# The first unit's row maxima over eight PSUM tiles, and the second unit's leading maxima ahead of the main loop

## The chip, the cores and the metric

One core of one Trainium2 chip runs the kernel. The metric is device time in microseconds (us), as the median of several executions; smaller is better. The engines are named as in the profile: PE (TensorE, matrix products, with PEld for its weight loads), DVE (VectorE), ACT (ScalarE), POOL (GpSimd) and SP (SyncE, which here only issues transfers). A queue such as ACTq or SPq is an engine's part that issues DMA transfers.

## The reference

Two independent results stand side by side in the output. `a` is a state-space convolution: a kernel `K` is made from 448 x 256 complex exponentials over 2048 positions, and the input is convolved with it. `b` is full attention with 16 heads of 28 columns over 2048 rows.

```python
K = 2.0 * jnp.einsum("dn,dnl->dl", C, P).real        # a: P = exp((A dt) l)
y = irfft(rfft(u_t, L2) * rfft(K, L2), L2)[:, :, :L] + u * D_skip

scores = jnp.einsum("bhqd,bhkd->bhqk", q, k) * scale  # b
p = softmax(scores, axis=-1)
b = (einsum("bhqk,bhkd->bhqd", p, v) ...) @ wo
out = jnp.concatenate([a, b], axis=-1)
```

## The kernel before

**Units and steps.** The 16 heads are four groups of four (`G`, `HG`), and the queries four blocks of 512 (`NQ`, `CQ`). A group with a query block is a unit `u`, 16 in all. The main loop (line 1045) has 256 steps `s`, 16 of them to a unit, one for each 128 keys (`kt`). A step makes for each of four heads a score tile (`s_mm`, line 753: a matmul into `pss`, then an exp on ACT into `p`), and adds the last step's `p` times `v` to the output tile `po` (`pv_step`, line 760).

**Row maxima.** An exp needs the largest score of its query row taken off beforehand. That maximum travels inside the matmul: two rows of the q tile `qhat` (one holds the rounded value, one the rest) hold minus the maximum, beside two rows of ones in `khat`. So a unit's maxima must be finished, and its row put into `qhat`, before the unit's first score matmul. A unit has 16 blocks `i`, each for one head `j` and 128 queries, and a block looks at 2048 keys in four columns `kc` of 512 (`max_mm`, line 187). For columns 0 and 1 a pair is used, max(a, b) = b + relu(a - b): `kc` 0 multiplies with the stored difference of keys, `kdif`, and ACT makes `rl`, the relu; `kc` 1 multiplies with the second half of the keys, and DVE adds `rl` and reduces in one operation. Columns 2 and 3 are matmuls that DVE reduces plainly.

For unit 0 alone, ahead of the loop, columns 2 and 3 are also a pair (`max_pair`, line 173). There is no stored difference for them, so two matmuls into one tile make it, the second with `q_neg`, minus the q tile, which ACT copies ahead of the first block (line 580). A block of unit 0 is then five matmuls, two relus and two pair reductions; a block of any other unit is four matmuls, one relu, one pair reduction and two plain ones.

After the last block `max_join` (line 208) takes the maximum over a block's values, `max_end` (line 212) transposes them on PE and splits them into the two rows `mh`, and `max_put` (line 220) sends these into `qhat` by two transfers, for unit 0 on ACT's queue.

**PSUM.** There are eight banks, one tile of 128 x 512 each. Before the loop they are divided into `ps_w` (3 tiles, `pm`, handed out in turn by `w_tile`, line 125), `ps_t` (2, `pt`), `ps_n` (2, `pn`) and `ps_x` (1, `px`); `pn` and `px` are used by the preparation of the convolution's seeds, whose last work ends at about 195 us. Unit 0's maxima use `pt` and `pm`, five tiles in turn (line 576). In the loop the banks are divided anew: `ps_s` (3, `pss`), `ps_o` (1), `ps_g` (1) and `ps_m` (3, again called `pm`). The relu results `rl` have two buffers, in the pool `kd_p`.

**The order of the work.** Up to line 590 the order of instructions on an engine comes from a scheduler, which starts from the order of the text and may let a later instruction go first. From line 903 on the text's order is kept on all engines (`nc.kept = KEPT["a"]`). There, first the seeds of three convolution blocks are loaded (`load_sd`, line 655; block 0 on ACT's queue, blocks 1 and 2 on SP's), then the first three (`LEAD`) blocks of unit 1's maxima are made (line 906), then ACT copies block 0's seeds `e` and `g` out of `sdb` (`k_seeds`, line 659), and the loop begins. The leading blocks give the loop its distance: step `s` makes the scores of its own unit and block `s + 16 + LEAD` of the maxima (line 1092), with the order in a step written out in `ORDER` (line 34): `m0`, `s0`, `m1`, `s1` and so on. POOL raises the powers of `e` (`e_power`, line 673), which PE multiplies with `g` some steps later (`k_mm`, line 712).

Of the kernel before, what the change touches and what calls it, by code (L numbers as in the profile page):

```python
# [8 lines left out]
F32 = mybir.dt.float32  # L9
F32R = mybir.dt.float32r  # L10
I32 = mybir.dt.int32
AF = mybir.ActivationFunctionType
# [11 lines left out]
HG = H // G  # L24
CQ = 512
# [7 lines left out]
LEAD = 3  # L33
# [57 lines left out]
def body(ctx, tc, a, out):  # L91
    nc = Engines(tc)
# [4 lines left out]
    def pool(stack, name, bufs=1, space=None, side=None):  # L97
        kw = {} if space is None else {"space": space}
        if side:
            kw["side"] = side  # L100
        return stack.enter_context(tc.tile_pool(name=name, bufs=bufs, reuse_waits="tile", **kw))
# [30 lines left out]
    kd_p = pool(att, "kd_p", side="right")  # L132
# [10 lines left out]
    kt_g, kd_g, q_u, m_u, mh_u, o_u, rl_u = {}, {}, {}, {}, {}, {}, {}  # L143
# [26 lines left out]
        for r in rows:  # L170
            nc.sync.dma_start(t[r::4].bitcast(F32), q_d[g][c][r // 2].rearrange("(j p) q -> p j q", j=HG))

    def max_pair(i, kc, ps, q_neg):
        j, t = divmod(i, 4)
        ts = slice(t * 128, (t + 1) * 128)
        pm, kt = ps(), kt_g[0][j]
        if kc == 2:
            nc.tensor.matmul(pm, q_u[0][:, j, ts], kt[:, 2 * CQ:3 * CQ], start=True, stop=False)
            nc.tensor.matmul(pm, q_neg[:, j, ts], kt[:, 3 * CQ:], start=False, stop=True)
            rl_u[0, i] = kd_p.tile([128, CQ], F32, name="rl", bufs=2)  # L180
            nc.scalar.activation(rl_u[0, i], pm, AF.Relu)
        else:
            nc.tensor.matmul(pm, q_u[0][:, j, ts], kt[:, 3 * CQ:], start=True, stop=True)
            rl = rl_u.pop((0, i))
            nc.vector.tensor_tensor_reduce(rl, pm, rl, 1.0, -3.0e38, ALU.add, ALU.max, m_u[0][:, j, t, 1:2])

    def max_mm(u, i, kc, ps=w_tile):

        if i == 0 and kc == 0:
            m_u[u] = q_p.tile([128, HG, 4, 3], F32, name="mx", bufs=2)  # L190
        j, t = divmod(i, 4)
        pm = ps()
        q, kt = q_u[u][:, j, t * 128:(t + 1) * 128], kt_g[u // NQ][j]
        mx = m_u[u][:, j, t, max(kc - 1, 0):max(kc - 1, 0) + 1]
        if kc == 0:
            nc.tensor.matmul(pm, q, kd_g[u // NQ, j], start=True, stop=True)
            rl_u[u, i] = kd_p.tile([128, CQ], F32, name="rl", bufs=2)
            nc.scalar.activation(rl_u[u, i], pm, AF.Relu)
        elif kc == 1:
            kb = kt.rearrange("p (c s n) -> p c s n", c=NQ, s=2)[:, :2, 1, :]  # L200
            nc.tensor.matmul(pm.rearrange("p (c n) -> p c n", c=2), q, kb, start=True, stop=True)
            rl = rl_u.pop((u, i))
            nc.vector.tensor_tensor_reduce(rl, pm, rl, 1.0, -3.0e38, ALU.add, ALU.max, mx)
        else:
            nc.tensor.matmul(pm, q, kt[:, kc * CQ:(kc + 1) * CQ], start=True, stop=True)
            nc.vector.tensor_reduce(mx, pm, axis=AX.X, op=ALU.max)

    def max_join(u, n=3):
        m_u[u, 1] = q_p.tile([128, HG * 4], F32, name="m1", bufs=2)
        nc.vector.tensor_reduce(m_u[u, 1], m_u[u].rearrange("p a b c -> p (a b) c")[:, :, :n], axis=AX.X, op=ALU.max)  # L210

    def max_end(u, ps):
        nc.tensor.transpose(ps[:16, :128], m_u[u, 1], ident)
        mh = q_p.tile([16, 2, 128], F32R, name="mh")
        nc.vector.tensor_scalar(mh[:, 0, :], ps[:16, :128], -1.0, None, op0=ALU.mult)
        nc.vector.scalar_tensor_tensor(mh[:, 1, :], ps[:16, :128], -1.0, mh[:, 0, :].bitcast(F32),
                                       op0=ALU.mult, op1=ALU.subtract)
        mh_u[u] = mh

    def max_put(u, queue=nc.sync):  # L220
        for i in range(2):
            queue.dma_start(q_u[u][4 * (DH + i):4 * (DH + i) + 1, :, :].rearrange("p h (t q) -> p (h t) q", t=4).bitcast(F32),
                                mh_u[u][:, i, :].bitcast(F32))


    with ExitStack() as st:
# [6 lines left out]
        ps_t = pool(st, "ps_t", 2, PSUM)  # L233
        ps_n = pool(st, "ps_n", 2, PSUM)
        ps_x = pool(st, "ps_x", 1, PSUM)
# [47 lines left out]
        half_pi = s_p.tile([128, 1], F32, name="half_pi")  # L283
# [289 lines left out]
                    load_v(0, c)  # L573
                kept_g.pop()()
        xst.close()
        more = [lambda: ps_t.tile([128, CQ], F32, name="pt")] * 2 + [w_tile] * 3
        n_st = ExitStack()
        q_neg = pool(n_st, "n_p").tile([128, HG, CQ], F32R, name="q_neg")
        for j in range(HG):
            nc.scalar.activation(q_neg[:, j], q_u[0][:, j].bitcast(F32), AF.Copy, scale=-1.0)  # L580
        for i in range(16):
            for kc in range(4):
                f, kw = (max_mm, (0, i, kc)) if kc < 2 else (max_pair, (i, kc))
                f(*kw, more[(4 * i + kc) % 5], *([q_neg] if kc > 1 else []))
        nc.scalar.activation(half_pi[:1], half_pi[:1], AF.Exp)
        n_st.close()
        max_join(0, 2)
        max_end(0, ps_t.tile([128, CQ], F32, name="pt"))
        max_put(0, nc.scalar)
        sst.close()  # L590


# [62 lines left out]
    def load_sd(b, queue=nc.sync):  # L655
        sds[b] = g_p.tile([128, SDF], F32, name="sdb", bufs=4)
        queue.dma_start(sds[b], sd_d[b // BO][b % BO])

    def k_seeds(b):

        if b not in es:
            es[b] = e = g_p.tile([128, 2, 16, N2], F32, name="e", bufs=2)
            nc.scalar.activation(e[:, :, :, :8], sds[b][:, :F_G].rearrange("p (c h e) -> p c h e", c=2, e=8), AF.Copy)
        else:
            g = g_p.tile([128, 2, 16, N1], F32, name="g", bufs=2)
            nc.scalar.activation(g[:, :, :, :4], sds[b][:, F_G:F_Z].rearrange("p (c h e) -> p c h e", c=2, e=4), AF.Copy)
            egs[b] = es.pop(b), g
# [235 lines left out]
    nc.kept = KEPT["a"]  # L903
    for b in range(3):
        load_sd(b, nc.sync if b else nc.scalar)
    for i in range(LEAD):
        for kc in range(4):
            max_mm(1, i, kc)
    k_seeds(0)
    k_seeds(0)  # L910

# [133 lines left out]
    for s in range(NS):  # L1045
# [25 lines left out]
        ps = []  # L1071
# [97 lines left out]
```

## Time and profile before

| what | value |
|---|---|
| median of 3 runs | 1283.33 us |
| lowest, highest | 1280.13, 1284.64 us |
| the profiled execution's own time | 1284.67 us |
| its span | 1282.8 us |
| PE busy | 1223.7 us, 95% of the span |
| DVE busy | 925.5 us, 72% |
| ACT busy | 967.8 us, 75% |
| POOL busy | 843.4 us, 66% |
| unit 0's pair reductions | from 196.04 to 224.87 us |
| unit 1's leading blocks on DVE | from 228.46 to 234.96 us |
| first score matmul | 234.41 us |

All times inside the profile count from the span's start; the time of the execution is a little longer than its span. A row of the timeline has the start, the duration, the engine, the operation with `out<-in` by the program's names, the number of merged instructions, and in brackets how long the engine had been idle and what ended that. A row of busy times by stretch has the stretch, then the busy time and the instructions of each engine, the clock that PE was granted as a share of the full one, and the share and rate of the DMA engines. An operation on DVE that also returns a maximum is two rows, CUSTOM_DVE_ANT_0 and a short DVE_READ_ACCUMULATOR2_ANT. Because a helper records every operation, all have the line 75, so tiles and engines tell them apart.

### The profile page before, as it was taken

The numbers are of one execution on the slowest core, as the hardware profiler recorded it, in microseconds if no ns is written. First come the engines' busy times: TensorE is split into PE (matmuls) and PEld (weight loads), VectorE is DVE, ScalarE is ACT, GpSimd is POOL, SyncE is SP. The second block draws the span as 40 slices with busy tenths as digits, with TensorE's granted clock in tenths as the row PEclk, the third lists the DMA queues.
The fourth block names the chain that finished last, engine by engine and source line by source line (L and its number), as shares of the span: only waits on it lengthen the run. The fifth ranks groups of instructions, "written<-read, shape, count | busy, mean of one in ns | idle before, by whom it ended". The sixth has DMA issues, their size and how long they took to land.

```text
span 1282.8 us, 33335 instructions
## 1 busy us (share of the span) xinstructions
PE 1223.7 (95%) x12641; PEld 700.9 (55%) x12641; DVE 925.5 (72%) x2106; ACT 967.8 (75%) x2162; POOL 843.4 (66%) x728
## 2 busy tenths in 40 slices
PE   7988867999999999999999999999999999999987
PEld 5867754455555555555555555555555555544433
DVE  5788877787877787878778888888887645645111
ACT  4978856688888888888888888888887666656452
POOL 2466651798778888877689999989995222324321
PEclk9988888899999999999999999999999999999999
DMA  6767887446664544465533223432324533657665
GB/s 210 263 242 241 265 301 290 127 93 182 172 154 106 156 133 146 128 214 195 169 102 91 61 76 106 149 88 71 83 59 154 175 135 132 205 171 227 194 171 165
DMA packets 200089, 205.36 MB, mean 160 GB/s; under 512 B 95992, under 2 KB 158520, under 8 KB 197880
## 3 DMA queue, kind: packets, MB, share of 16 engines
q1 hardware_dynamic: 199720, 202.87, 51.4%
q8 instruction: 100, 1.64, 0.5%
q10 hardware_dynamic: 208, 0.36, 0.1%
q14 instruction: 61, 0.50, 0.1%
HBM read 120.73 MB, written 82.18 MB: 158 GB/s over the span
## 4 chain that ended last, share of the span: by engine, by line
PE 77%; DVE 7%; ACT 5%; POOL 5%; issue 3%; DMA 2%; SPq 0%; ACTq 0%; POOLq 0%; DVEq 0%
PE pm L75 44%; PE pss L75 16%; PE po L75 16%; POOL e L75 1%; ACT tri L75 1%; DVE mx L75 1%; ACT rl L75 1%; PE pt L75 1%; POOL qhat L75 1%; DVE sg L75 1%; DVE hl L75 1%; DVE tri L75 1%; POOL x_e L75 1%; DVE px L75 1%; POOL p L75 1%
## 5 line engine op out<-in xcount | busy, mean ns | idle before, releaser
L75 ACT ACTIVATE p<-pss 128x512 f32<-128x512 f32 x1024 | 561.4, 611 | 112.8 <-PE pss L75 108.5
L75 PE MATMUL pss<-qhat,khat 128*128 128x512 f32 x1024 | 402.7, 399 | 1.5 <-ACT p L75 1.4
L75 DVE TENSOR_REDUCE mx<-pm 128x1 f32<-128x512 f32 x480 | 308.6, 684 | 109.6 <-PE pm L75 107.5
L75 PE MATMUL pm<-khat,qhat 128*128 128x512 f32 x749 | 326.4, 439 | 5.3 <-ACT rl L75 3.0
L75 POOL TENSOR_TENSOR e<-e,sdb 128x256 f32<-128x256 f32 x168 | 201.9, 1202 | 108.1 <-ACT e L75 62.4
L75 PE MATMUL po<-p,v 128*32 128x512 f32 x2048 | 269.1, 594 | 0.0
L75 POOL TENSOR_TENSOR e<-e,eu 128x256 f32<-128x256 f32 x168 | 248.0, 1476 | 13.2
L75 PEld LDWEIGHTS pm<-khat,qhat 128*128 128x128 f32 x749 | 141.4, 189 | 201.3 <-ACT p L75 52.0
L75 DVE CUSTOM_DVE_ANT_0 rl<-pm,rl 128x512 f32<-128x512 f32 x259 | 178.4, 689 | 71.6 <-ACT rl L75 68.4
L75 PEld LDWEIGHTS pss<-qhat,khat 128*128 128x128 f32 x1024 | 190.4, 188 | 46.1 <-issue 10.8
L75 POOL TENSOR_TENSOR eu<-e,sdb 128x256 f32<-128x256 f32 x168 | 202.0, 1202 | 0.0
L75 POOL TENSOR_TENSOR p<-pr,pr 64x448 f32<-64x448 f32 x64 | 73.1, 1142 | 160.4 <-PE pm L75 135.2
L75 ACT ACTIVATE rl<-pm 128x512 f32<-128x512 f32 x259 | 157.1, 607 | 12.7 <-PE pm L75 7.9
L75 DVE TENSOR_TENSOR g<-g,zg 128x128 f32<-128x128 f32 x392 | 162.2, 414 | 3.4
L75 PE MATMUL pm<-kdif,qhat 128*128 128x512 f32 x249 | 101.1, 406 | 8.5 <-DVE xn L75 6.6
L75 PE MATMUL pm<-xh,khat 112*128 112x512 f32 x256 | 87.0, 422 | 9.2 <-DVE kb L75 4.4
L75 DVE TENSOR_TENSOR zg<-g,zg 128x128 f32<-128x128 f32 x224 | 87.9, 393 | 5.1
L75 PEld LDWEIGHTS pm<-e,g 128*32 128x32 f32 x3584 | 57.2, 109 | 43.8 <-issue 16.1
L75 DVE TENSOR_TENSOR pr<-pm,ub 128x448 f32<-128x448 f32 x64 | 37.0, 620 | 56.2 <-PE pm L75 41.8
L75 PE MATMUL pm<-e,g 128*32 128x64 f32 x3584 | 73.0, 222 | 1.9 <-POOL e L75 1.9
L75 ACT ACTIVATE y<-pm 128x448 f32<-128x448 f32 x48 | 26.5, 553 | 58.2 <-PE pm L75 34.1
L75 ACT ACTIVATE ub<-pm 128x224 f32<-128x224 f32 (+1 forms) x96 | 38.8, 450 | 39.9 <-PE pm L75 37.6
(134 smaller groups left out, 1465.5 us busy)
## 6 DMA issues: line engine op xcount, KB each, us to landing
sdb<-sd SPq DMA_DIRECT2D x55, 336.0 KB
qhat<-q SPq DMA_DIRECT2D x64, 256.0 KB
khat<-k SPq DMA_DIRECT2D x64, 256.0 KB
sd<-sg SPq DMA_DIRECT2D x8, 1456.0 KB
k<-hl SPq DMA_DIRECT2D x16, 512.0 KB
mw<-in_mw SPq DMA_DIRECT2D x16, 512.0 KB
sd<-qhat SPq DMA_DIRECT2D x8, 896.0 KB
yu_d<-ub SPq DMA_DIRECT2D x64, 112.0 KB
```

The source lines that it names most:

```text
L75: i = f(*args, **kw)
```

## The change

Unit 0's maxima go over all eight PSUM tiles instead of five, in the order `pt`, `pm`, `pt`, `pm`, `pn`, `pm`, `pn`, `px`, and a block's columns are taken in the order 0, 2, 1, 3 instead of 0, 1, 2, 3, so that both relus come ahead of both reductions. The relu buffers of columns 2 and 3 get a place of their own: three in the pool of `q_neg` (`n_p`), beside the two in `kd_p` that columns 0 and 1 and unit 1 use. The text of unit 0's end (join, transposition, row) now stands ahead of unit 1's three leading blocks, which leave the part whose order is kept (line 906) and come before line 590, over the same eight tiles; the pool of `q_neg` closes after them. The seed loads, which stood ahead of the leading blocks, now follow them in the text.

```diff
-    def max_pair(i, kc, ps, q_neg):
+    def max_pair(i, kc, ps, q_neg, rl_p):
...
-            rl_u[0, i] = kd_p.tile([128, CQ], F32, name="rl", bufs=2)
-            nc.scalar.activation(rl_u[0, i], pm, AF.Relu)
+            rl_u[0, i, 1] = rl_p.tile([128, CQ], F32, name="rl", bufs=3)
+            nc.scalar.activation(rl_u[0, i, 1], pm, AF.Relu)
...
-        more = [lambda: ps_t.tile([128, CQ], F32, name="pt")] * 2 + [w_tile] * 3
+        p_t, p_n, p_x = (lambda p=p, n=n: p.tile([128, CQ], F32, name=n) for p, n in ((ps_t, "pt"), (ps_n, "pn"), (ps_x, "px")))
+        more = [p_t, w_tile, p_t, w_tile, p_n, w_tile, p_n, p_x]
...
         for i in range(16):
+            for n, kc in enumerate((0, 2, 1, 3)):
+                ps = more[(4 * i + n) % 8]
+                max_mm(0, i, kc, ps) if kc < 2 else max_pair(i, kc, ps, q_neg, n_p)
+        nc.scalar.activation(half_pi[:1], half_pi[:1], AF.Exp)
+        max_join(0, 2)
+        max_end(0, p_t())
+        max_put(0, nc.scalar)
+        for i in range(LEAD):
             for kc in range(4):
-                f, kw = (max_mm, (0, i, kc)) if kc < 2 else (max_pair, (i, kc))
-                f(*kw, more[(4 * i + kc) % 5], *([q_neg] if kc > 1 else []))
-        nc.scalar.activation(half_pi[:1], half_pi[:1], AF.Exp)
+                max_mm(1, i, kc, more[(4 * i + kc + 1) % 8])
         n_st.close()
-        max_join(0, 2)
-        max_end(0, ps_t.tile([128, CQ], F32, name="pt"))
-        max_put(0, nc.scalar)
...
     for b in range(3):
         load_sd(b, nc.sync if b else nc.scalar)
-    for i in range(LEAD):
-        for kc in range(4):
-            max_mm(1, i, kc)
     k_seeds(0)
```

More of the change, by code (lines that the diff above doesn't have):

```diff
@@ L179, in max_pair @@
             nc.tensor.matmul(pm, q_neg[:, j, ts], kt[:, 3 * CQ:], start=False, stop=True)
-            rl_u[0, i] = kd_p.tile([128, CQ], F32, name="rl", bufs=2)
-            nc.scalar.activation(rl_u[0, i], pm, AF.Relu)
+            rl_u[0, i, 1] = rl_p.tile([128, CQ], F32, name="rl", bufs=3)
+            nc.scalar.activation(rl_u[0, i, 1], pm, AF.Relu)
         else:
             nc.tensor.matmul(pm, q_u[0][:, j, ts], kt[:, 3 * CQ:], start=True, stop=True)
-            rl = rl_u.pop((0, i))
+            rl = rl_u.pop((0, i, 1))
             nc.vector.tensor_tensor_reduce(rl, pm, rl, 1.0, -3.0e38, ALU.add, ALU.max, m_u[0][:, j, t, 1:2])
@@ L575, in body @@
         xst.close()
-        more = [lambda: ps_t.tile([128, CQ], F32, name="pt")] * 2 + [w_tile] * 3
+        p_t, p_n, p_x = (lambda p=p, n=n: p.tile([128, CQ], F32, name=n) for p, n in ((ps_t, "pt"), (ps_n, "pn"), (ps_x, "px")))
+        more = [p_t, w_tile, p_t, w_tile, p_n, w_tile, p_n, p_x]
         n_st = ExitStack()
-        q_neg = pool(n_st, "n_p").tile([128, HG, CQ], F32R, name="q_neg")
+        n_p = pool(n_st, "n_p")
+        q_neg = n_p.tile([128, HG, CQ], F32R, name="q_neg")
         for j in range(HG):
```

## The prediction

> **What bounds the kernel now.** I read the page first, for the chain of work that ended last and the groups, then the busy times by stretch, then the timelines of DVE, PE and ACT around 195 to 235 us, where the changed lines run.
>
> ```profile
> PE 77%; DVE 7%; ACT 5%; POOL 5%; issue 3%; DMA 2%; SPq 0%; ACTq 0%; POOLq 0%; DVEq 0%
> ...
> L75 PE MATMUL pm<-e,g 128*32 128x64 f32 x3584 | 73.0, 222 | 1.9 <-POOL e L75 1.9
> ```
>
> 77% of the chain is TensorE's own work. The second row matters below: in the whole run PE waited 1.9 us for GpSimd's powers. All operations stand under the helper's line, 75, so I go by tiles.
>
> ```profile
> core 0: us, PE busy (x) PEld busy (x) DVE busy (x) ACT busy (x) POOL busy (x), PEclk, DMA share, GB/s
> 196.06:203.30 7.24, 6.98 (x15) 4.38 (x15) 4.10 (x13) 5.46 (x10) 0.76 (x1) 0.50 1.02 391
> 203.30:224.90 21.60, 18.03 (x62) 10.13 (x60) 17.35 (x52) 14.30 (x25) 0.00 (x0) 0.99 0.66 234
> 224.90:234.40 9.50, 7.10 (x14) 3.64 (x15) 5.88 (x15) 2.30 (x5) 1.08 (x2) 0.64 0.65 208
> 234.40:300.00 65.60, 65.46 (x685) 34.65 (x687) 53.47 (x126) 55.22 (x123) 58.32 (x47) 1.00 0.43 110
> 300.00:960.00 660.00, 655.64 (x7866) 366.28 (x7859) 543.41 (x1296) 553.41 (x1272) 572.17 (x450) 1.00 0.44 125
> ```
>
> From 234.40 us on, the main loop, PE is busy 65.46 of 65.60 us and then 655.64 of 660 at a granted clock of 1.00, in an order written out by hand. So the loop has a length of its own, and whatever lets it begin earlier ends the kernel earlier by as much. The change touches only the three stretches before it: the first unit's maxima while PE's clock is at 0.50 (7.24 us), the same at full clock (21.60 us, no engine full), and the passage to the loop (9.50 us), where no engine is full at the clock it could have.
>
> ```profile
> 196.04 0.69 DVE L75 CUSTOM_DVE_ANT_0 rl<-pt,rl 128x512 f32<-128x512 f32 x1 [1.06 <-ACT rl L75]
> ...
> 203.29 0.69 DVE L75 CUSTOM_DVE_ANT_0 rl<-pm,rl 128x512 f32<-128x512 f32 x1 [0.58 <-ACT rl L75]
> ...
> 206.80 0.69 DVE L75 CUSTOM_DVE_ANT_0 rl<-pt,rl 128x512 f32<-128x512 f32 x1
> 207.41 0.08 DVE L75 DVE_READ_ACCUMULATOR2_ANT mx<- 128x1 f32 x1
> 207.83 0.69 DVE L75 CUSTOM_DVE_ANT_0 rl<-pm,rl 128x512 f32<-128x512 f32 x1 [0.34 <-ACT rl L75]
> ...
> 224.18 0.69 DVE L75 CUSTOM_DVE_ANT_0 rl<-pm,rl 128x512 f32<-128x512 f32 x1 [0.34 <-ACT rl L75]
> 224.79 0.08 DVE L75 DVE_READ_ACCUMULATOR2_ANT mx<- 128x1 f32 x1
> 224.91 0.19 DVE L75 TENSOR_REDUCE m<-mx 128x16 f32<-128x32 f32 x1
> 225.55 0.28 DVE L75 TENSOR_SCALAR mh<-pt 16x128 fp32r<-16x128 f32 x1 [0.45 <-PE pt L75]
> 225.86 0.28 DVE L75 SCALAR_TENSOR_TENSOR mh<-pt,mh 16x128 fp32r<-16x128 f32 x1
> 228.46 0.69 DVE L75 CUSTOM_DVE_ANT_0 rl<-pm,rl 128x512 f32<-128x512 f32 x1 [2.32 <-ACT rl L75]
> 229.08 0.08 DVE L75 DVE_READ_ACCUMULATOR2_ANT mx<- 128x1 f32 x1
> 229.08 1.28 DVE L75 TENSOR_REDUCE mx<-pm 128x1 f32<-128x512 f32 x2
> ```
>
> The custom operation is the reduction of a pair (max of pm plus rl): 32 of them for unit 0, two for each of 16 blocks, the first at 196.04, the seventh at 203.29, the 32nd at 224.18. Where the next is ready, one follows after 0.61 us (206.80 to 207.41); but the one after that waits 0.34 us for ACT's rl. From the seventh to the 32nd it is (224.18 - 203.29) / 25 = 0.84 us for each. At 228.46 unit 1's three leading blocks begin, one pair reduction and two plain reductions (1.28 us) each.
>
> ```profile
> 206.77 0.39 PE L75 MATMUL pm<-khat,q_neg 128*128 128x512 f32 x1
> 207.00 0.40 PE L75 MATMUL pt<-khat,qhat 128*128 128x512 f32 x1
> ...
> 228.48 0.79 PE L75 MATMUL pm<-khat,qhat 128*128 128x512 f32 x1 [2.05 <-ACT rl L75]
> ...
> 234.41 0.41 PE L75 MATMUL pss<-qhat,khat 128*128 128x512 f32 x1
> ```
>
> ```profile
> 225.91 1.25 ACTq L75 DMA_DIRECT2D qhat<-mh  x2
> 227.19 0.59 ACTq L75 DMA_DIRECT2D sdb<-sd  x1
> 227.83 0.60 ACT L75 ACTIVATE rl<-pm 128x512 f32<-128x512 f32 x1 [3.69 <-DMA qhat<-mh]
> ...
> 232.84 0.41 ACT L75 ACTIVATE e<-sdb 128x256 f32<-128x256 f32 x1
> ...
> 235.11 1.09 ACT L75 ACTIVATE p<-pss 128x512 f32<-128x512 f32 x2
> ```
>
> ACT stood 3.69 us idle while it held the row's two transfers and the first seed's load ahead of the leading blocks' first rl. I measure the passage from the 32nd pair reduction, L = 224.18: row issued at L+1.7, seed load at L+3.0, first leading rl at L+3.65, first leading reduction at L+4.3, first score matmul at L+10.2, first exp at L+10.9.
>
> **The change, part by part.**
>
> *Eight tiles and the order 0, 2, 1, 3.* Nothing is added or removed: 80 matmuls, 32 rl, 32 pair reductions as before. Full-clock matmuls follow each other after 0.23 us (206.77 to 207.00), five a block, 1.17 us; DVE needs 2 x 0.61 = 1.22; ACT's rl take 0.60, two a block 1.20. All three are below the 1.68 us (2 x 0.84) that a block takes now, so the time goes in waiting for a tile or an rl buffer to come back. With eight tiles a block's tile is wanted again two blocks later, 2.4 us, and the chain matmul 0.40, rl 0.60, reduction 0.69 is 1.7: it fits. The rl buffers go from two in all to two and three. The floor is DVE's 0.61 a reduction; with three engines within 5% of one another I don't expect the floor. 0.72, the middle of 0.61 and 0.84, is the other end; I take 0.65, nearer the floor. From the seventh reduction, 203.29 + 25 x 0.65 = 219.54: **4.6 us earlier** (5.6 at the floor, 2.9 at 0.72). Before the seventh I expect no gain: at clock 0.50 five matmuls take twice 1.17 us, 2.3, PE is busy 6.98 of 7.24 us, and the start waits on ACT behind the seeds, which the diff leaves alone.
>
> *q_neg stays where it is; the relu buffers move to its pool*, which closes after the leading blocks instead of before the row. No instruction; the readers of those buffers are done by L+0.7 either way, ahead of everything that takes their place. Cost nothing; without that cover at most one reduction, 0.69.
>
> *The leading blocks ahead of the loop.* Twelve matmuls, three rl, nine reductions, no DMA. They are moved past the row's ACT transfers, past the load of seed 0 (ACT queue) and seeds 1 and 2 (SP), and past nothing on POOL. In the part where they now stand the order on an engine isn't held to the text. That such reordering happens shows in a row: the Exp that loads the table is written behind the first unit's blocks and ran long ahead of them.
>
> ```profile
> L75 ACT ACTIVATE half_pi<-half_pi x1: 202/202/202, 179.6 to 179.6; 1x1 f32<-1x1 f32 x1
> ```
>
> So I expect the three rl ahead of the row's transfers, which only become ready at L+1.7. DVE then has: last reduction 0.7, join 0.2, row 0.56, and 3 x 0.61 + 3 x 1.28 = 5.7 of leading reductions, together L+7.2, no longer L+4.3 + 5.7. A reduction that stands ahead of the row's two operations delays the row by 0.7 at most, and behind the row waits only the first score matmul, which has slack: issued at L+1.7, it released ACT 1.9 us later (225.91 to 227.83), so it is there at L+4.3.
>
> What is late next is seed 0. Its load is issued at L+3.0 as now. ACT takes e and g from it ahead of the loop's first rl and exp, in the written order, so all exps queue behind that landing. Bounds for the landing: 1.9 us after issue as with the row, or 5.65, since at 232.84 e ran without a wait. Middle 3.8: L+6.8. Then e 0.41, g 0.3 at most 0.41 like e, rl 0.60, 1.3 together: first exp at L+8.1 instead of L+10.9, **2.8 us** (1.0 to 4.7 between the bounds). POOL's first power follows e, which stands 2.3 us ahead of the first exp now and 1.3 then, 1.0 later against the loop; PE waited 1.9 us for powers in the whole run, and I set the cost at nothing, 1.9 if that cover goes.
>
> *The loop's first tiles* take the banks of the leading blocks; the last reader is done at L+7.2, before the first exp. Nothing, or one plain reduction, 0.64.
>
> Sum: 4.6 + 2.8 = **7.4 us**. The profiled execution itself took 1284.67 us (span 1282.8), 1.3 above the median; its own time would become 1277.3, and the median 1283.33 becomes **1275.9**.
>
> *The clock.* In the rows the clock is 0.50 for 7.24 us although PE is busy for 6.98 of them, and an idle gap of 2.05 us at 228.48 stands in a stretch that averages 0.64; yet at 234.40 the clock is 1.00. After the change PE has its twelve leading matmuls done early and then waits for the tiles, the row and exp, so the loop's first steps could fall into a slow stretch.
> [...]
>
> **The rivals.**
>
> A. *ACT keeps the written order*: row transfers, then the three rl. The third rl needs the first buffer back at L+5.0, seed 0's load goes out at L+5.6, lands at L+9.4, first exp L+10.7. Gain 4.6 + 0.2: 1278.5. For it: the ACT rows above; against: the table's Exp.
>
> B. *The loop begins at clock 0.50.* PE is then the bound and each such us loses half: up to 7.24 / 2 = 3.6. 1275.9 to 1279.5, most likely about 1278. For it: the 0.64 row; against: 1.00 at 234.40 after a stretch with about as many matmuls as the new one.
>
> C. *The tiles weren't the limit*, so the change doesn't do what it says: ACT, at 1.20 of 1.22 us, passes each delay on, and 0.84 stays. Gain 2.8 only: 1280.5.
>
> D. *Slower.* The freedom that lets the rl go ahead lets a leading matmul go ahead on PE's queue of the first unit's, and it needs unit 1's q.
>
> ```profile
> 205.02 3.44 SPq L75 DMA_DIRECT2D qhat<-q  x4
> ```
>
> Those four loads end issuing at 208.46 and land, by the row's 1.9, at 210.4 or later. A leading matmul placed at 198.0, two microseconds behind the first reduction, would hold PE 12.4 us; less the 7.4, 5.0 us slower: 1288.3. It decides up to 199.1: a later place gives a loss within 0.3%, and one behind 203.0 a gain. Against it: sixteen blocks stand in front in the text, and each freed tile is wanted by one of them first.
>
> E. *More*: with eight tiles PE doesn't stall in the slow stretch and gets its clock half of it, 3.6 us, sooner: 1.6 blocks become 2.8, 1.2 x 1.3 = 1.6 us more, 1274.3.
>
> **How the numbers follow.** Forecast 0.47, A 0.10, B 0.15, C 0.11, D 0.09, E 0.08. A difference of 0.3%, 3.85 us, is about what a measurement of this kernel can tell from no change, so faster means below 1279.5: forecast, A, E and 0.11 of B, 0.76. Same: C and the rest of B, 0.15. Slower: D, 0.09. The bounds alone give gains of 2.9 + 1.0 = 3.9 (1279.4) to 5.6 + 4.7 = 10.3 (1273.0). The range goes down to 1271.5 for E on top of these, and up to 1281.5 to take in C with 1 us of the runs' spread; D is left out.
>
> **What would show it.** Pair reductions of unit 0 about 0.65 us apart from the seventh on and the 32nd near 219.5; no wait of 3.7 us on ACT at the row; the first leading reduction within 1.5 us of the 32nd; first exp near 227.6 and e<-sdb just ahead of it; clock 1.00 from there. Wrong would make it: a 32nd reduction later than 222, leading rl behind the row's transfers (A), 0.50 in the loop's first 7 us (B), a score matmul or a first-unit matmul waiting for q (D), or a loop longer than now by more than 1 us from first exp to end.

## The result, and the profile after

The changed kernel takes 1278.63 us (median of 20 runs, 1276.68 to 1283.24), the kernel before, in 20 runs beside it, 1282.09. The ratio is 0.998, 95% interval 0.9973 to 0.9987: 2.6 us gained (1.7 to 3.5), where 7.4 were forecast. The ratio is taken over all the runs; the two medians alone lie 3.5 us apart. The profiled execution took 1278.61 us, its span is 1276.8. The kernel before took 1284.67 us in its profiled execution, 2.6 above its median, so the two profiles lie further apart than the runs.

I split both spans at the same four events. T1 and L are the starts of the first and the 32nd pair reduction of unit 0 (L as in the prediction). Exps are counted from 0, so exp 8 is the first of the loop's third step (the expectations call it the eighth).

| stretch, us | before | after | difference |
|---|---|---|---|
| start to T1 | 196.04 | 194.39 | -1.65 |
| T1 to L (unit 0) | 28.14 | 23.81 | -4.33 |
| L to exp 0 | 10.94 | 11.45 | +0.51 |
| exp 0 to exp 8 | 5.51 | 5.96 | +0.45 |
| exp 8 to the end | 1042.18 | 1041.20 | -0.98 |

I don't count the first and the last row to the change. T1 follows ACT's last work for the seeds (`sg`, at 195.01 before and 193.36 after), and ACT's order ahead of T1 is the same; PE makes some of unit 0's matmuls earlier, into `pn` and `px`. T1 spreads from 192.79 to 194.77 in ten profiles with the changed kernel's unit 0, from 192.94 to 196.04 in five with the old order. The last row's difference lies within the spread of all the profiles (1040.55 to 1043.40). So of the 6.0 us between the two spans 3.4 lie where the change works. Unit 0 gave about what was forecast (4.6), though not where it was forecast; the passage to the loop, forecast 2.8 shorter, became a little longer.

The busy times by stretch come next, first after, then before, split where the granted clock changes:

```profile
194.39:197.64 3.25, 3.25 (x7) 1.93 (x7) 2.62 (x7) 2.03 (x4) 0.78 (x1) 0.50 1.00 379
197.64:224.94 27.30, 21.86 (x80) 13.34 (x78) 21.92 (x69) 18.67 (x35) 0.00 (x0) 1.00 0.77 266
224.94:231.77 6.83, 4.36 (x10) 3.38 (x11) 4.40 (x11) 3.12 (x8) 2.47 (x4) 0.50 0.85 252
231.77:300.00 68.23, 67.92 (x752) 36.12 (x754) 54.72 (x130) 56.85 (x126) 61.61 (x49) 1.00 0.42 104
```

```profile
196.04:203.71 7.67, 7.39 (x16) 4.70 (x17) 4.53 (x13) 5.48 (x10) 0.78 (x1) 0.50 1.03 391
...
227.60:234.43 6.83, 5.95 (x11) 3.08 (x12) 5.16 (x12) 2.30 (x5) 1.11 (x2) 0.50 0.90 289
```

In both a stretch of 6.83 us at clock 0.50 lies at the passage. Before, it ended at 234.43, 0.7 us ahead of the first exp (235.11), so the loop ran at full clock. After, the first exp is at 229.65 and the half clock lasts until 231.77: it has moved into the loop.

The timeline of DVE, ACT and PE in the passage after the change:

```profile
218.20 0.69 DVE L75 CUSTOM_DVE_ANT_0 rl<-px,rl 128x512 f32<-128x512 f32 x1
...
221.84 0.69 DVE L75 CUSTOM_DVE_ANT_0 rl<-pt,rl 128x512 f32<-128x512 f32 x1 [1.68 <-ACT rl L75]
...
226.68 0.68 DVE L75 TENSOR_REDUCE mx<-pn 128x1 f32<-128x512 f32 x1
```

```profile
219.93 1.24 ACTq L75 DMA_DIRECT2D qhat<-mh  x2
221.21 1.09 ACT L75 ACTIVATE rl<-pm 128x512 f32<-128x512 f32 x2 [4.07 <-PE pn L75]
222.64 0.60 ACT L75 ACTIVATE rl<-pm 128x512 f32<-128x512 f32 x1 [0.34 <-DVE mx L75]
222.66 0.35 ACTq L75 DMA_DIRECT2D sdb<-sd  x1
228.65 0.42 ACT L75 ACTIVATE e<-sdb 128x256 f32<-128x256 f32 x1 [5.42 <-DMA sdb<-sd]
...
229.65 1.08 ACT L75 ACTIVATE p<-pss 128x512 f32<-128x512 f32 x2
```

```profile
219.26 0.27 PE L75 MATMUL pt<-ident,m 128*16 128x128 f32 x1 [2.26 <-DVE m L75]
219.50 0.47 PE L75 MATMUL pm<-kdif,qhat 128*128 128x512 f32 x1
...
223.80 0.50 PE L75 MATMUL pn<-khat,qhat 128*128 128x512 f32 x1
227.41 0.80 PE L75 MATMUL pm<-kdif,qhat 128*128 128x512 f32 x1 [3.11 <-DVE mx L75]
228.00 0.63 PE L75 MATMUL pss<-qhat,khat 128*128 128x512 f32 x1
228.43 0.63 PE L75 MATMUL pm<-khat,qhat 128*128 128x512 f32 x1
```

L is 218.20. These rows show three holds, one behind another. **The row**: ACT issues the row's transfers at 219.93 and only then the leading blocks' first rl (221.21); and on PE the twelve leading matmuls stand behind the transposition, which waits for the join. The leading reductions run from L+3.6 to L+9.2, not from about L+1 to L+7.2. **The bank**: the loop's first matmul (227.41) had waited 3.11 us for DVE, until the last leading reduction (226.68 and 0.68 long) freed its bank. **The seed**: its load goes out at 222.66 behind the third leading rl, and e, which stands ahead of every exp, waits for it until 228.65, 6.0 us behind the issue.

### The profile page after: what moved, and what is told of

The parts are those of the page before. It is cut to its first block, busy times and chain, and to the rows that moved or that the text cites. A ratio compares the mean times of both kernels' runs of the same rounds, so it can differ in the third digit from the quotient of the medians.

```text
span 1276.8 us, 33338 instructions
## 1 busy us (share of the span) xinstructions
PE 1219.3 (95%) x12641; PEld 699.8 (55%) x12641; DVE 925.3 (72%) x2106; ACT 966.9 (76%) x2162; POOL 843.5 (66%) x728
## 4 chain that ended last, share of the span: by engine, by line
PE 77%; DVE 9%; ACT 4%; POOL 4%; issue 3%; DMA 2%; ACTq 0%; SPq 0%; POOLq 0%; DVEq 0%
PE pm L75 43%; PE pss L75 17%; PE po L75 16%; POOL qhat L75 1%; DVE mx L75 1%; DVE sg L75 1%; ACT tri L75 1%; DVE px L75 1%; DVE tri L75 1%; POOL x_e L75 1%; DVE hl L75 1%; DVE qhat L75 1%; PE pt L75 1%; DVE rl L75 1%; POOL p L75 1%
## 5 line engine op out<-in xcount | busy, mean ns | idle before, releaser
L75 PE MATMUL pm<-khat,qhat 128*128 128x512 f32 x737 | 320.2, 435 | 6.1 <-DVE mx L75 1.7
L75 PEld LDWEIGHTS pm<-khat,qhat 128*128 128x128 f32 x737 | 138.6, 188 | 198.2 <-ACT p L75 45.3
L75 DVE CUSTOM_DVE_ANT_0 rl<-pm,rl 128x512 f32<-128x512 f32 x245 | 168.8, 689 | 67.3 <-ACT rl L75 65.2
L75 PE MATMUL pm<-kdif,qhat 128*128 128x512 f32 x240 | 95.9, 400 | 4.2 <-DVE mx L75 3.1
```

The source lines that it names most:

```text
L75: i = f(*args, **kw)
```

## The experiments

Each kernel ran five to twelve times, beside 21 to 26 runs of the kernel before on the same chip (its medians 1281.25 to 1281.64). Ratios are to that kernel. Unit 0 is T1 to L, and exps count from L; both come from one profiled execution of each kernel, and executions of one kernel lie up to 6.7 us apart. With the row on SP alone the profiled execution was the slowest of seven (1279.81 us, median 1276.99), with all three edits the fastest of five (1273.58, median 1275.09).

| run | ratio (95%) | unit 0 | exp 0 | exp 8 |
|---|---|---|---|---|
| kernel before | 1 | 28.14 | 10.94 | 16.45 |
| changed kernel | 0.998 (0.9973 to 0.9987) | 23.81 | 11.45 | 17.41 |
| unit 0's part alone | 0.9973 (0.9962 to 0.9985) | 25.84 | 10.96 | 16.49 |
| the same, five tiles | 0.9977 (0.9968 to 0.9986) | 25.05 | 10.96 | 16.84 |
| eight tiles, old order, two rl buffers | 0.9969 (0.9957 to 0.998) | 24.28 | 10.96 | 16.96 |
| the move alone | 1.0005 (0.9996 to 1.0014) | 27.60 | 11.50 | 17.09 |
| change + seed early | 0.998 (0.997 to 0.999) | 25.78 | 10.54 | 17.65 |
| change + row on SP | 0.9966 (0.9953 to 0.9979) | 25.81 | 10.20 | 17.25 |
| change + banks dealt | 0.9981 (0.997 to 0.9991) | 24.05 | 11.33 | 19.13 |
| change + row, seed | 0.9977 (0.9968 to 0.9986) | 23.74 | 9.33 | 16.64 |
| change + seed, banks | 0.9956 (0.994 to 0.9973) | 24.04 | 8.90 | 16.64 |
| change + row, banks | 0.997 (0.996 to 0.998) | 25.82 | 10.53 | 17.21 |
| change + row, seed, banks | 0.9948 (0.9936 to 0.9961) | 23.84 | 7.65 | 13.40 |
| move + row, seed, banks | 0.9977 (0.9967 to 0.9987) | 27.35 | 7.15 | 13.71 |

**The two parts apart.** Theory: unit 0's part carries the gain, and the move gives nothing because the holds above take its place. Rival: both are half as good as forecast. First unit 0's part with the leading blocks back behind the seed loads (the edit is against the changed kernel), then the move with unit 0 as before (against the kernel before; lines left out at the dots):

```diff
-        for i in range(LEAD):
-            for kc in range(4):
-                max_mm(1, i, kc, more[(4 * i + kc + 1) % 8])
...
+    for i in range(LEAD):
+        for kc in range(4):
+            max_mm(1, i, kc)
     k_seeds(0)
```

> Only the first part: unit 0 over eight tiles, the leading blocks back in the kept part behind the seed loads. Theory (the leading blocks' move gave nothing, because their relus stood behind the row's transfers on ACT and seed 0 landed later): first to last pair reduction of unit 0 takes 23.8 us as in the changed kernel (28.1 before), last reduction to first exp 10.9 as before; 3.8 to 4.3 us faster than before, so no worse than the changed kernel. Rival (the move gave its 2.8 us and the loop lost it again): 11.4 or more to the first exp and a slower time than the changed kernel by about 2 to 3 us.

```diff
-        n_st.close()
...
+        more = [p_t, w_tile, p_t, w_tile, p_n, w_tile, p_n, p_x]
+        for i in range(LEAD):
+            for kc in range(4):
+                max_mm(1, i, kc, more[(4 * i + kc + 1) % 8])
+        n_st.close()
...
-    for i in range(LEAD):
-        for kc in range(4):
-            max_mm(1, i, kc)
     k_seeds(0)
```

> Only the second part: unit 0 over five tiles as before, the three leading blocks ahead of the loop over eight tiles. Theory: 28 us for unit 0; last reduction to first exp about 11.4 instead of 10.9, the loop's first matmuls at half clock, so 0.5 to 1 us slower than before, within noise. Rival (the move gives a gain of its own): up to 2.8 us faster.

Measured: 1277.76 us against 1281.25, 3.5 us gained (1.9 to 4.9), and 1281.9, nothing. So unit 0's part alone gives what the whole change gives, and the move's 2.8 us are missing completely.

**What held unit 0: tiles or rl buffers?** One run goes back to five tiles and keeps the new order and five rl buffers (the edit is against unit 0's part alone); the other has eight tiles with the old order and two rl buffers (against the kernel before). In both the leading blocks stay where they were.

```diff
-        more = [p_t, w_tile, p_t, w_tile, p_n, w_tile, p_n, p_x]
+        more = [p_t, p_t, w_tile, w_tile, w_tile]
...
-                ps = more[(4 * i + n) % 8]
+                ps = more[(4 * i + n) % 5]
```

> Unit 0 in the new column order and with the five relu buffers, but over five tiles as before; the leading blocks stay where they were. Theory (relu buffers): before, the two shared buffers set the pitch, 2 x 0.84 us a block being a relu of 0.60, a reduction of 0.69 and the hand-overs between; with five of them five tiles are enough. From the 1st to the 32nd pair reduction about 25.8 us as with unit 0's part alone (23.8 if PE keeps its clock at the copies of q_neg), pitch 0.61 to 0.68 in the last ten, time about 1277.8 beside 1281.3 for the kernel before. Rival (tiles): five tiles hold the pitch near 0.8, 27.5 to 28.1 us, time about 1281.

```diff
-        more = [lambda: ps_t.tile([128, CQ], F32, name="pt")] * 2 + [w_tile] * 3
+        more = [p_t, w_tile, p_t, w_tile, p_n, w_tile, p_n, p_x]
...
-                f(*kw, more[(4 * i + kc) % 5], *([q_neg] if kc > 1 else []))
+                f(*kw, more[(4 * i + kc) % 8], *([q_neg] if kc > 1 else []))
```

> Unit 0 over eight tiles, but in the old column order and with the two shared relu buffers; the leading blocks stay where they were. Theory (relu buffers): the pitch stays near 0.84, 27.5 to 28.1 us from the 1st to the 32nd pair reduction, DVE goes on waiting about 0.34 us for ACT's rl at every second reduction, time about 1281 beside 1281.3 for the kernel before. Rival (tiles): pitch 0.61 to 0.68 and 25.8 us or less, time about 1277.8.

Measured: 1278.73 and 1277.61 against 1281.64; unit 0 in 25.05 and 24.28 us. Each half alone removes the 0.84 us pitch (from the 7th to the 32nd reduction 0.72 and 0.73). My theory, that the two buffers alone set it, is refuted, and so is its rival in the sharp form: five tiles alone don't set it either. The run with five tiles had the new order as well as the five buffers, so which of these two helped it isn't shown. The DVE timeline of the run with two buffers shows what they still cost, 0.62 and 0.80 in turn, where the changed kernel's later reductions stand 0.61 apart:

```profile
205.55 0.69 DVE L75 CUSTOM_DVE_ANT_0 rl<-px,rl 128x512 f32<-128x512 f32 x1
...
206.17 0.69 DVE L75 CUSTOM_DVE_ANT_0 rl<-pm,rl 128x512 f32<-128x512 f32 x1
...
206.97 0.69 DVE L75 CUSTOM_DVE_ANT_0 rl<-pm,rl 128x512 f32<-128x512 f32 x1
...
207.59 0.69 DVE L75 CUSTOM_DVE_ANT_0 rl<-pm,rl 128x512 f32<-128x512 f32 x1
```

Over eight tiles with five buffers unit 0 took 23.7 to 25.8 us, so it is hardly faster than in these two runs. One reason shows in the changed kernel's timelines of ACT, DVE and PE:

```profile
200.21 2.18 ACT L75 ACTIVATE q_neg<-qhat 128x512 fp32r<-128x512 f32 x4
```

```profile
200.34 0.69 DVE L75 CUSTOM_DVE_ANT_0 rl<-pn,rl 128x512 f32<-128x512 f32 x1
...
202.91 0.69 DVE L75 CUSTOM_DVE_ANT_0 rl<-pm,rl 128x512 f32<-128x512 f32 x1 [1.86 <-ACT rl L75]
```

```profile
202.93 0.50 PE L75 MATMUL pm<-khat,qhat 128*128 128x512 f32 x1 [1.31 <-ACT rl L75]
```

In the changed kernel eight rl, the columns 0 of eight blocks, go ahead of the copies of `q_neg`, so these stop the pairs in the middle of the run: 2.56 us between the eighth and the ninth reduction. The kernel before has the same stop at the start, 2.64 us between the first (196.04) and the second. Its ACT and DVE rows:

```profile
195.90 2.17 ACT L75 ACTIVATE q_neg<-qhat 128x512 fp32r<-128x512 f32 x4
```

```profile
198.68 0.69 DVE L75 CUSTOM_DVE_ANT_0 rl<-pm,rl 128x512 f32<-128x512 f32 x1 [1.94 <-ACT rl L75]
```

So the change moved the stop from ahead of the seventh reduction to behind it. From the first to the seventh it took 5.23 us instead of 7.25, from the seventh to the 32nd 18.59 instead of 20.89.

**One hold at a time.** Theory: row, seed and bank each hold the passage, so taking away one lets the next decide. Rival: one of them is the whole loss. The edits are the same in all runs that follow:

```diff
 # seed early: into a tile of its own, loaded before unit 0
+                sd0 = pool(sd_st, "sd_p", side="right").tile([128, SDF], F32, name="sdf")
...
+                nc.sync.dma_start(sd0, sd_d[0][0])
...
-    for b in range(3):
-        load_sd(b, nc.sync if b else nc.scalar)
+    sds[0] = sd0
+    for b in range(1, 3):
+        load_sd(b)
 # row on SP
-        max_put(0, nc.scalar)
+        max_put(0)
 # banks dealt: the banks of the loop's first tiles get early readers
+        lead = [p_t, p_t, w_tile, p_x, w_tile, p_n, p_x, p_n, w_tile, w_tile, p_t, p_t]
-                max_mm(1, i, kc, more[(4 * i + kc + 1) % 8])
+                max_mm(1, i, kc, lead[4 * i + kc])
```

> The changed kernel, but seed 0 is loaded into a tile of its own long before, on SP's queue. Theory (the exps queue behind seed 0's landing): ACT no longer waits 5.4 us for it, first exp is bound by the first score matmul and comes 9.9 to 10.4 us after the last reduction instead of 11.45, so 1 to 1.5 us faster than the changed kernel. Rival (the landing is covered by the score matmul, which comes just as late): no change.

> The changed kernel with unit 0's row sent on SP's queue instead of ACT's. Theory: ACT doesn't stand before the leading blocks' relus; the first comes 1.8 us after the last reduction instead of 3.0, DVE is done with the leading blocks 1.2 us earlier, seed 0 is issued at 3.3 instead of 4.5; 1.2 to 2.5 us faster than the changed kernel, more where the store of the last seeds no longer shares the queue's time with seed 0. Rival (the relus wait for PE, which waits for the row's transposition, not for the transfers): under 0.5 us.

> The changed kernel with only the leading blocks' tiles dealt so that the loop's first banks have early readers; the row stays on ACT's queue and the seed's load behind the leading blocks. Theory (in the changed kernel the seed's landing holds the exps at L+11.4, whatever the banks do): first exp at L+11 to L+11.5, the loop's first m0 early, so that the eighth exp comes 5 to 6 us behind the first; at most 0.5 us gained, 1278 to 1278.7 where the kernel before takes 1281.5. Rival (the bank that the last leading reduction holds is the whole loss): 3 us gained as with all three edits, about 1275.5.

Measured: 1278.99, 1276.99 and 1278.99. In its profile none brings exp 8 nearer to L than the kernel before has it (17.65, 17.25, 19.13 against 16.45). The row on SP has the best ratio of the three, but its interval overlaps the changed kernel's. With the early seed the next hold is the bank, as the timelines of DVE and PE show: PE is idle for 3.12 us, and goes on as the last leading reduction (229.03 to 229.71) ends. The bracket names a transfer that had long been issued; the time fits DVE.

```profile
229.03 0.68 DVE L75 TENSOR_REDUCE mx<-pn 128x1 f32<-128x512 f32 x1
```

```profile
226.15 0.49 PE L75 MATMUL pn<-khat,qhat 128*128 128x512 f32 x1
229.76 0.80 PE L75 MATMUL pm<-kdif,qhat 128*128 128x512 f32 x1 [3.12 <-DMA sd<-sg]
```

With the row on SP the first leading rl goes at L+2.1 instead of L+3.0, but the seed holds again. ACT's timeline:

```profile
224.59 0.38 ACTq L75 DMA_DIRECT2D sdb<-sd  x1
228.79 0.42 ACT L75 ACTIVATE e<-sdb 128x256 f32<-128x256 f32 x1 [3.62 <-DMA sdb<-sd]
```

With the dealt banks alone the seed holds as in the changed kernel (exp 0 at L+11.33).

**Two at a time.**

> The whole change, with the row's two transfers on SP's queue and the first seed loaded early into a tile of its own. Theory (ACT's row and the seed's landing hold the passage; behind them the loop's first tile waits for the last leading reduction): leading reductions from L+2.7 to L+8.3 as with the row on SP alone, no wait for the seed, the loop's first m0 at L+8.3, the first exp 1.3 us behind it as with the early seed alone: L+9.6, against 10.2 and 10.5 with one of the two. Time 0.5 us below the row on SP alone: about 1276.5 where the kernel before takes 1281.3. Rival (the loop's first steps make up for any later start, so the end doesn't follow the first exp): no difference from the row on SP alone, 1277.0.

> The changed kernel with the early seed and the dealt banks, the row left on ACT's queue. Theory (each of the three is a hold of its own, and the next one takes over when one is gone): the leading reductions start at L+3.6 as in the changed kernel, 1.0 later than with the row on SP; the loop's first score matmul follows the third leading block's bank, so the first exp comes 1.0 to 1.5 later than with all three, L+8.7 to L+9.2, and PE is idle so much longer that a half-clock stretch can fall on the loop's start. Eighth exp at L+14.5 to L+16.5, ratio to the kernel before 0.9955 to 0.9965. Rival (the row's queue doesn't matter, seed and banks are all): eighth exp at L+13.4, ratio 0.995.

> The changed kernel with the row on SP's queue and the dealt banks, the first seed loaded where it was. Theory: the seed's landing holds all exps as with the row on SP alone, first exp at L+10.2, half clock at the loop's start, eighth exp at L+16.5 to L+17.5, ratio to the kernel before 0.9966 to 0.998. Rival (the banks are all): eighth exp at L+13.4, ratio 0.995.

Measured: 1279.13, 1275.85 and 1278.27. The first exp comes nearer to L step by step (9.33, 8.90, 10.53), but exp 8 is at 16.64, 16.64 and 17.21. I had expected half a us less than the row alone from row and seed; there was none. The row-and-banks run went as expected. In the seed-and-banks run time and profile don't quite agree: its exp 8 stands where the kernel before has it, but its ratio, 0.9956, is nearer to that of all three edits below. Its six runs lie between 1273.0 and 1279.66, and the interval reaches from the full gain to half of it, so how much of the gain these two edits hold without the row stays open.

**All three.**

> As the last one, and the leading blocks' tiles are dealt so that the loop's first score and m0 banks have early readers. Theory (the last leading reduction's bank holds the loop's first matmul): the first matmuls of the loop run from about L+5 to L+6, when the row has landed, the first exp at L+6 to L+7.5, but the loop's DVE work still starts behind the leading reductions at L+8.3, so that two thirds of it are given back by exp 64; 1 us gained at the end, about 1275.5 where the kernel before takes 1281.3. Rival (DVE alone decides from the leading reductions on): first exp earlier, but the end as in the last one, 1276.5.

Measured: 1275.09 against 1281.64, ratio 0.9948 (0.9936 to 0.9961), 6.7 us gained. This version beats both kernels: its interval lies wholly below the changed kernel's, though it overlaps those of the row alone and of two of the pairs. PE and ACT in its passage (L is 217.85):

```profile
224.96 0.51 PE L75 MATMUL pss<-qhat,khat 128*128 128x512 f32 x1 [1.06 <-DVE mx L75]
225.30 0.40 PE L75 MATMUL pm<-khat,qhat 128*128 128x512 f32 x1
225.54 0.40 PE L75 MATMUL pss<-qhat,khat 128*128 128x512 f32 x1
```

```profile
225.50 1.13 ACT L75 ACTIVATE p<-pss 128x512 f32<-128x512 f32 x2 [0.97 <-PE pss L75]
```

The matmuls stand 0.24 apart, where those of the changed kernel's first steps stand 0.43 apart (228.00 to 228.43). So in these profiles the three edits together gave two things: an earlier exp 0, and a loop that starts at full clock. As this execution was the fastest of five, the others may have lost some of the clock.

**The half clock by itself.** Is it a cause of its own, or a companion? To the row-and-seed version I added eight matmuls into an idle bank, ahead of the loop; nobody reads them.

```diff
+        warm = p_x()
+        for i in range(8):
+            nc.tensor.matmul(warm, q_u[0][:, 0, :128], kd_g[0, 0], start=True, stop=True)
         n_st.close()
```

> Row on SP and early seed as in that experiment, with eight more matmuls into an idle bank (px) ahead of the loop; nobody reads them. Theory (the loop's first step at clock 0.50 takes back 1.3 to 1.8 us, because PE stood idle for 3.1 us in front of it): clock 1.00 from the loop's start, the eighth exp 5.5 to 6 us behind the first where it was 7.3, the first exp at L+9.3 as it was, 1.3 to 1.8 us below that experiment: ratio to the kernel before about 0.9965. Rival (the eighth exp is late for another reason, the order of DVE's and ACT's work behind the leading reductions): still 7.3 us, no gain, ratio 0.9977.

Measured: 1279.18, ratio 0.9978 (0.9968 to 0.9988), no gain: my expectation missed. PE's timeline says why:

```profile
224.43 3.24 PE L75 MATMUL px<-kdif,qhat 128*128 128x512 f32 x8 [1.97 <-DVE mx L75]
227.47 0.63 PE L75 MATMUL pm<-kdif,qhat 128*128 128x512 f32 x1
...
228.62 0.40 PE L75 MATMUL pss<-qhat,khat 128*128 128x512 f32 x1
```

The bank was free later than I had taken, so most of the eight ran at half clock themselves, 3.24 us, and the first exp moved to L+11.06. But from there the theory's other half came out: full clock from 228.46, and exp 8 came 5.52 us behind exp 0, not 7.31. With all three edits, also at full clock, it came 5.75 behind. So the half clock at the loop's start costs 1.6 to 1.8 us between these profiles; this way of avoiding it costs as much. The busy times by stretch of row and seed (first two rows), seed and banks (third) and all three (fourth) show PE's load in the windows ahead of it:

```profile
221.59:225.00 3.41, 1.53 (x5) 0.52 (x3) 3.41 (x9) 1.16 (x4) 1.93 (x3) 1.00 0.96 291
225.00:231.82 6.82, 5.50 (x16) 3.88 (x20) 4.42 (x12) 4.04 (x8) 6.62 (x5) 0.50 0.66 171
```

```profile
220.42:223.83 3.41, 1.71 (x7) 0.86 (x5) 3.38 (x8) 1.59 (x5) 1.52 (x3) 1.00 0.74 257
```

```profile
221.19:224.61 3.42, 2.00 (x8) 1.00 (x6) 3.42 (x9) 2.21 (x5) 1.75 (x3) 1.00 0.81 256
```

Windows of 3.41 us at full clock with five and seven matmuls (1.53 and 1.71 us busy) were followed by 6.8 us at 0.50; one with eight (2.00) was not. The rows also count matmuls that reach in from before; 3, 5 and 6 began in these windows. The seed-and-banks run differs from all three only in the row's queue: its exp 0 is 1.25 later, and a further 2.0 us are gone by exp 8.

**Is the move worth its 2.8 us?** Unit 0 as before, with the move and the three edits:

> Unit 0 as before (five tiles, old order, two relu buffers); the leading blocks moved as in the change, with row on SP, early seed and dealt banks. The move alone made no difference (ratio 1.0005). Theory (the move is worth its 2.8 us once row, seed and banks don't hold the passage): eighth exp at L+13.4 to L+14.5 instead of L+16.45, 2 to 3 us gained, ratio 0.9976 to 0.9984; unit 0 in 27.6 to 28.1 us. Rival (what the passage gains is given back in the loop's first 64 exps): 64th exp as far behind L as before, 71.5 us, ratio 1.000.

Measured: 1278.57 against 1281.3, ratio 0.9977 (0.9967 to 0.9987), 2.9 us gained; exp 8 at L+13.71, 2.74 nearer than before, and exp 64 at L+68.88, not 71.48: next to nothing is given back. With unit 0's own ratio, 0.9973 x 0.9977 = 0.995, about what all three gave on the whole change (0.9948). But this is the move and the three edits together. No run gave the edits to a kernel without the move, and there the row's queue could matter as well: in the kernel before ACT began to issue the row at 225.91 and made its first leading rl only at 227.83, 1.9 us later. How much of the 2.9 us is the move's own stays open.

**Old order of the columns.** Can the stop at `q_neg` be removed as well? All three edits, with the columns in the order 0, 1, 2, 3:

> The version with row on SP, early seed and dealt banks, but with the columns of a block in the old order 0, 1, 2, 3 (eight tiles and the relu buffers of the change stay). Theory (the new order costs PE a stop at the copies of q_neg, 2.56 us between two reductions, since four blocks' first relus go ahead of the copies; with the old order eight tiles gave a pitch of 0.72 from the second reduction on and no such stop): unit 0 from the 1st to the 32nd pair reduction in 21 to 22.5 us instead of 23.8, passage as it was (first exp L+7.7, no half clock), 1.5 to 2.5 us below it: about 1273 where the kernel before takes 1281.5, ratio 0.993 to 0.994. Rival (the stop only moves to another place): 23.8 us again, ratio 0.995.

Measured: 1275.35 against 1281.31, ratio 0.9947 (0.9933 to 0.9961), no better than 0.9948. The stop only moved ahead (2.76 us, between the fourth and the fifth reduction), though unit 0 became 1.1 us shorter, 22.76. Its profile has clock 0.50 from 223.46 to 226.87 and exp 8 at L+15.02. Whether the order or the phase of the clock's windows lost that, one profile can't say.

## Why the prediction was wrong, point by point

*What bounds the kernel*: right. From exp 8 to the end all the profiles lie between 1040.55 and 1043.40 us, whatever went ahead; the two above 1042.2 have one more half-clock window near 1230 to 1239.

*Eight tiles, 4.6 us*: right in mechanism, mis-sized. Unit 0's part measured 3.5 us (1.9 to 4.9), 4.33 in the two profiles compared. That this is so near 4.6 is in part luck. The pitch of the last sixteen is 0.616, the floor I didn't expect; but the moved stop of 2.56 us now lies among the 25, so that they gained 2.3 us, not 4.6. The other 2.0 came ahead of the seventh, where I expected none: the stop is no longer there. And the profile of the kernel before has the longest unit 0 of the three with its tiles and order (28.14; the others 27.60 and 27.35), while the changed kernel's is one of the shorter: in four of ten profiles the stop also cost a window of full clock, and unit 0 took 25.8 instead of 23.7 to 24.1 us. The means, 27.7 and 24.7, are 3.0 apart. Rival C is refuted.

*The leading blocks ahead of the loop, 2.8 us*: **this is the step that failed**, and its first sentence failed first: "so I expect the three rl ahead of the row's transfers". The Exp that ran ahead had its data long before; the leading rl had not. Their matmuls stood behind the transposition on PE, so the rl became ready no sooner than the row. This is rival A's order, to which I gave 0.10; its first exp at L+10.7 is near what came. That its 1278.5 us is near as well is luck: it is 4.8 below a median that was 1283.33 then and 1282.09 in the runs beside the changed kernel, and 2.6 were gained.

*Seed 0*: the landing took 6.0 us behind its issue at L+4.5, not 3.8 behind L+3.0; my bounds were 1.9 and 5.65. I had named it as what is late next, with the wrong size.

*The loop's first tiles, nothing*: wrong. As soon as the seed is early, they hold the loop (3.12 us of idle PE). In the changed kernel the seed covers them. The leading reductions ended at L+9.2, not L+7.2; but with row and seed gone they ended at L+7.95, and the bank still cost 1.7 us (exp 0 at L+9.33, with dealt banks 7.65). What I had missed is that not the first exp but the loop's first matmul needs the bank, and it stands 1.3 us ahead of that exp.

*The clock, rival B*: it came true as well, in the same run as A. I had weighed them as exclusive; but A's wait empties PE ahead of the loop, and the half clock followed. That the one brings on the other is argued. Together they are more than the missing 2.8 us: exp 0 at L+11.45 instead of L+8.1, then 0.45 more by exp 8 than in the kernel before, 3.8 in all.

*Rivals D and E*: D didn't come; the first leading matmul ran at 219.50, behind all of unit 0's. E can't be told from chance: the half clock ended 3.25 us behind T1 instead of 7.67, but over the ten profiles with the changed kernel's unit 0 it ended 3.1 to 6.1 behind it, and 5.7 to 7.7 in the five with the old order. That PE gets its clock back sooner when it doesn't stall was an assumption of mine that no run shows: in the kernel before, PE was busy for 7.39 of the last 7.67 us at clock 0.50.

*The sum*: 7.4 lies near what the change gives with the three edits (6.7, interval 5.0 to 8.2), and the move with the edits gave 2.74 us in the profile, about its term; what the move would give without any hold and without the edits isn't shown. That row, seed and bank hold one behind another is shown in the profiles: no edit alone and no two brought exp 8 nearer to L than the kernel before has it (16.64 at best against 16.45), all three did (13.40). The times bear this out more loosely, as the intervals of the row alone and of seed and banks reach that of all three. That the half clock goes with PE's emptier window is seen in the rows above, but no run set PE's load in one window and changed nothing else.

## What to carry to other kernels

When a stage ends on several waits close together, write them down in their order with times: taking away the latest gains only the distance to the next, and much of the gain can come with the last of them. Here the Exp went ahead because its data were there, and the leading rl didn't because theirs were not; so follow the queue of an instruction's inputs, not its own alone, before counting on a new order. And look which banks the next stage takes over, and deal them so that their last readers are early.

## What the runs showed of the hardware that was not expected

**In these profiles the clock went by windows of 3.41 us, with a phase that differed from one to the next.** In the sixteen profiles the half-clock stretches from 179 us to the loop last 3.41, 6.83, 10.24, 17.07 or 20.48 us, all multiples of 3.413 (20.48 / 6). (The prediction's 7.24 us was a window that I chose; the half-clock stretch around it lasts from 183.23 to 203.71, six windows.) Where the windows begin differs from profile to profile, and the same stop at `q_neg` cost a window in some and none in others. From 195 us to the loop, windows at full clock in which four or fewer matmuls began were always followed by a half-clock one (10 of 10), those with seven or more never (none of 13 in the profiles of the kernel before and the changed kernel). With five it was 10 of 12, with six 1 of 6 (some records may be missing). Busy time alone draws no line, as the window ahead of the changed kernel's loop shows, which a half-clock stretch followed although PE counts as busy for 2.05 us of it:

```profile
221.53:224.94 3.41, 2.05 (x5) 0.74 (x4) 3.10 (x8) 1.37 (x3) 0.00 (x0) 1.00 0.66 207
```

**The same load of 336 KB landed after 4.0 to 4.2 us or after 5.9 to 6.0.** In the changed kernel, where it took 6.0, SP issued the 896 KB store of the last seeds (`sd<-qhat`) just ahead of the loads:

```profile
221.88 0.36 SPq L75 DMA_DIRECT2D sd<-qhat  x1
222.29 1.70 SPq L75 DMA_DIRECT2D sdb<-sd  x2
```

In the two runs with the row on SP and the seed where it was, that store had gone at 207 to 209 us, and the seed landed 4.2 and 4.0 us behind its issue. The other two loads also left 1.2 us or more ahead of the seed there, where in the changed kernel one left 0.4 us ahead of it and the other behind it. That the store is the reason is argued; no run moved it alone.
